# Routed attention and two expert layers: three early steps of the first heads moved to other slots

## Chip, cores and metric

The kernel is one program on one core of a Trainium2 chip. The metric is device time in microseconds (us) of that core; the median of three timed runs of the kernel before is 674.37 us (673.11 to 674.87).

## What is computed

Inputs are q, k, v of shape (2, 8, 768, 64), 16 centroids for each of the 8 heads, and the weights of two expert layers. The part that the change touches is the attention:

```python
q_assign = argmax(normalize(q) @ normalize(centroids), axis=-1)     # a cluster for each row
k_assign = argmax(normalize(k) @ normalize(centroids), axis=-1)
mask   = q_assign[:, :, :, None] == k_assign[:, :, None, :]
scores = where(mask, q @ k.T / 8, -1e9)
scores = scores - max(scores, axis=-1)
attn   = exp(scores) / (sum(exp(scores)) + 1e-9)
out    = attn @ v                                                    # (2, 8, 768, 64)
```

The result, as 1536 tokens of 512 values, then goes through an expert layer with a skip gate and through one with a capacity (8 experts of 512 x 1024 x 512 each). Everything is float32.

## The kernel before, in words

**Tiles.** The 16 (batch, head) pairs are worked as 8 groups g of two heads; head numbers h run from 0 to 15. For a group, `load` (line 108) brings q and k to SBUF (tile `qkn`) and `load_V` (line 123) brings v (tile `vn`); both tiles come from a pool with two buffers, so group 2 gets the buffers of group 0 once every reader of them is done. `prep_T` (128) transposes q and k on TensorE into `qkT`; `prep_H` (153) and `prep_L` (161) split `qkT` into a high part `qkH` and a low part `qkL`, which have one buffer each (pool `wrk`): a group can't write them before all readers of the group ahead are done. For group 1 `prep_H` is on ScalarE and `prep_L` on GpSimd; for groups from 2 on `prep_T` itself writes `qkH` on ScalarE (line 149). `prep_V` (167) splits v: a ScalarE copy to `VA` (line 172) and a GpSimd subtraction to `VL` (line 173), both reading `vn`.

**Stacking.** `stack_q(g, h, t)` (242) copies pieces of `qkH` and `qkL` from SBUF to SBUF into the operands `AA` and `BB` of one head, four DMAs for t = 0 and, for group 0, four more for t = 1 (three for later groups). They are issued by SyncE, but for (0, 1, 0), which GpSimd issues. `stack_mk` does the same for the mask rows.

**Heads.** `mpass(h, c)` (265) computes the row maxima of one block of 128 rows from the t = 0 half of `AA` and `BB`: two matmuls (line 271) and two VectorE reductions (272), and after block 5 one more (274). `mrow(h)` (276) transposes the maxima on TensorE (278) and writes them as rows into `BB` (279), from where `score_mm` (282, matmuls of line 290) subtracts them. `score` (293) takes the exponential on ScalarE (298), splits it (299 on ScalarE, 301 on GpSimd, two buffers for `P`), and `pv` (304) multiplies with `VA` and `VL`.

**Order.** All is put into a table of slots by `at(u, step, ...)`: slot u stands for score block u of 96 (6 for a head), negative slots are the preparation. Slots are emitted in rising u, and within one slot in the order in which `at` was called. The order of TensorE, SyncE, GpSimd and ScalarE is the emitted one throughout; VectorE's is the emitted one up to slot 6 (lines 451 and 452) and is chosen by a planner after that. Each engine works through its instructions in order, and a DMA on SyncE's queue whose condition isn't met holds back all DMAs behind it.

The early slots are: -40 the loads of q and k of groups 0 and 1; -20 the two loads of v and then the whole preparation of group 0, ending with `prep_V(0)`; -10 to -3 the preparation of group 1 (`prep_H` in -6, -5, -4; `prep_L` in -6, -5, -3) beside the row maxima of head 0 (`mpass(0, c)` in slots -8 to -3); -8 also the loads of group 2 (`load(2)`, then `load_V(2)`); -3 also `mrow(0)`; -2 `prep_V(1)`; 0 the first scores. Slot 1 has the stacking of group 1 and slot 3 `prep_mk(1)` (line 239), `stack_mk(1)` and the first `prep_T(2)`.

Of the kernel before, what the change touches and what calls it, by code (L numbers as in the profile page):

```python
# [22 lines left out]
def attention(ctx, tc, q, k, v, centroids, wcat, lgacc, xa, xb, idw, hooks, bind):  # L23
# [354 lines left out]
    def at(u, fn, *a):  # L378
        sched.setdefault(u, []).append((fn, a))
# [1 line left out]
    NH = 2 * NP  # L381
    LM = 8
    MP = (0, 1, 2, 3, 4, 4)
    lead = {1: (-3, -1, -1, 1, 3, 3), 2: (6, 8, 7, 8, 7, 9)}
    for u in range(NH * C):
        h, c = divmod(u, C)
        at(u, score_mm, h, c)
# [21 lines left out]
    for g in range(NP):  # L409
        u = 2 * C * g  # L410
        if g > 1:
            at(u + -32, load, g)
            at(u + -32, load_V, g)
        if g == 0:
            at(-20, load_V, 0)
            at(-20, load_V, 1)
            for x in ((prep_T, 0, 0), (cen_T,), (prep_H, 0, 0), (prep_L, 0, 0), (prep_T, 0, 1), (prep_H, 0, 1), (prep_L, 0, 1),
                      (prep_T, 0, 2), (prep_H, 0, 2), (prep_as, 0, 0), (prep_as, 0, 1), (stack_q, 0, 0, 0), (stack_q, 0, 1, 0),
                      (next, su), (prep_oh, 0, ((0, 1),)), (prep_as, 0, 2), (warm, 5), (prep_mk0, 0), (prep_oh, 0, ((1, 2),)),
                      (prep_L, 0, 2), (warm, 4), (prep_mk0, 1), (warm, 1), (stack_q, 0, 0, 1), (stack_q, 0, 1, 1),  # L420
                      (prep_V, 0)):
                at(-20, *x)
        else:
            w = (-10, -7, -7) if g == 1 else [u + x for x in (-21, -20, -18)]
            for i in range(3):
                at(w[i], prep_T, g, i)
            if g == 1:
                for i, (l, h) in enumerate(zip((-6, -5, -3), (-6, -5, -4))):
                    at(h, prep_H, g, i)
                    at(l, prep_L, g, i)  # L430
            w = (-5, -4, -3) if g == 1 else [u + x for x in (-19, -17, -16)]
            for i in range(3):
                at(w[i], prep_as, g, i)
            w = -1 if g == 1 else u + -14
            at(w, prep_oh, g)
            w = 3 if g == 1 else u + -12
            at(w, prep_mk, g)
            for h in range(2):
                x = 1 if g == 1 else w + 0
                at(x, stack_q, g, h, 0)  # L440
                at(x, stack_q, g, h, 1)
                at(w, stack_mk, g, h)
        if g:
            at(u + -10 if g > 1 else -2, prep_V, g)
        at(u + 2 * C + -3, fin_w, g)
        at(u + 2 * C + 4, fin_den, g)
        at(u + 2 * C + 4, fin_nat, g, 0)
        at(u + 2 * C + 5, fin_nat, g, 1)
# [1076 lines left out]
def tile_kernel(ctx, tc, q, k, v, centroids, moe_w_skip, moe_w_gate, moe_w1, moe_w2,  # L1525
# [6 lines left out]
    with tc.manual_schedule(engines={ET.PE, ET.SP, ET.Pool, ET.Activation}):  # L1532
# [46 lines left out]
        with ExitStack() as actx:  # L1579
            moe.at = actx.enter_context(tc.tile_pool(name="mat", bufs=1))  # L1580
            attention(actx, tc, q, k, v, centroids, wcat, lg, xa, xb, idw, hooks, bind)
# [34 lines left out]
```

## Time and profile before

| | |
|---|---|
| median of three timed runs | 674.37 us |
| the profiled execution, its own time | 678.05 us |
| span of its instructions | 676.3 us |
| mean granted TensorE clock | 0.988 |
| TensorE matmuls busy | 639.2 us (95%) |
| TensorE weight loads busy | 553.2 us (82%) |
| VectorE busy | 419.3 us (62%) |
| ScalarE busy | 379.9 us (56%) |
| GpSimd busy | 264.9 us (39%) |
| DMA, SyncE's queue | 108.18 MB, 52.5% of 16 engines' span |

In the profile PE is TensorE's matmuls and PEld its weight loads, DVE is VectorE, ACT ScalarE, POOL GpSimd and SPq the DMA issues of SyncE. A line of the timeline gives start and duration in us, engine, source line, operation and `out<-in` tiles, and a count where several are merged; in brackets stands how long the engine was idle before and what ended that. The busy shares are means over stages with different limits: the change lies in the first 45 us, and there the stage itself has to be read.

### The profile page before, as it was taken

Reading aid. Unit: us, or ns where it says so; the run is one execution under the profiler, and the core shown is the slowest. Engines: PE = TensorE matmul, PEld = TensorE weight load, DVE = VectorE, ACT = ScalarE, POOL = GpSimd, SP = SyncE. Lnnn points to the kernel's source line nnn. Section 1 sums busy time; section 2 is a strip of 40 time slices with the busy share of each in tenths; the row PEclk is TensorE's granted clock in tenths of the full one; section 3 lists DMA queues with packets and bytes.
Section 4 is the critical chain, followed back from the end, with each engine's and each line's share of the span. In section 5 each row is a group of like instructions: output and inputs, shape, how many; then the busy total and the mean of one; then the engine's idle time right before and its main releaser. Section 6 shows DMA issues by size and latency. Waiting matters only on the chain. (4 is left out here: it accounts for less than half of the span.)

```text
span 676.3 us, 11848 instructions
## 1 busy us (share of the span) xinstructions
PE 639.2 (95%) x4238; PEld 553.2 (82%) x4238; DVE 419.3 (62%) x1027; ACT 379.9 (56%) x626; POOL 264.9 (39%) x194
## 2 busy tenths in 40 slices
PE   7889999999998999999999999997999999999994
PEld 6768888888877888887788899985799889888984
DVE  6958666676678775344867765647454865646421
ACT  4767787878776779841443434323344645546440
POOL 6665776767665688801211112003013212302210
PEclk9899999999998999999999999999999999999998
DMA  8973838484824479420687888941495476367100
GB/s 230 207 145 90 203 85 202 84 201 88 203 63 90 107 176 372 129 77 27 186 317 276 314 321 319 336 152 48 157 389 188 180 277 241 134 244 257 34 32 3
DMA packets 78960, 121.49 MB, mean 180 GB/s; under 512 B 27569, under 2 KB 42929, under 8 KB 78896
## 3 DMA queue, kind: packets, MB, share of 16 engines
q1 hardware_dynamic: 74416, 108.18, 52.5%
q0 software_dynamic: 4480, 12.50, 5.5%
q8 instruction: 35, 0.57, 0.3%
q14 instruction: 29, 0.24, 0.1%
HBM read 87.90 MB, written 13.37 MB: 150 GB/s over the span
## 5 line engine op out<-in xcount | busy, mean ns | idle before, releaser
L301 POOL TENSOR_TENSOR Pl<-P,Ph 128x768 fp32r<-128x768 f32 x93 | 170.3, 1841 | 70.7 <-ACT Ph L299 36.2
L983 DVE TENSOR_TENSOR wl<-l,wh 128x1024 fp32r<-128x1024 f32 x92 | 109.3, 1221 | 51.3 <-ACT wh L982 50.4
L272 DVE TENSOR_REDUCE m<-psx 128x1 f32<-128x384 f32 x192 | 98.0, 551 | 34.4 <-PE psx L271 33.1
L290 PE MATMUL pss<-BB,AA 128*128 128x384 f32 (+1 forms) x384 | 88.9, 355 | 10.4 <-ACT P L298 3.8
L298 ACT ACTIVATE P<-pss 128x384 f32<-128x384 f32 x192 | 84.0, 489 | 24.8 <-PE pss L290 19.8
L982 ACT CAST wh<-l 128x1024 fp32r<-128x1024 f32 x92 | 92.3, 1046 | 0.5 <-DVE acco L1143 0.5
L299 ACT CAST Ph<-P 128x768 fp32r<-128x768 f32 x96 | 80.1, 835 | 4.2 <-PE pso L318 1.2
L1005 PE MATMUL psl<-xt,l 128*128 128x128 f32 x640 | 79.3, 280 | 1.0 <-ACTq L1209 1.0
L290 PEld LDWEIGHTS pss<-BB,AA 128*128 128x128 f32 (+1 forms) x384 | 66.7, 192 | 16.4 <-ACT P L298 5.2
L1005 PEld LDWEIGHTS psl<-xt,l 128*128 128x128 f32 x640 | 76.2, 195 | 2.4 <-ACTq L1209 1.3
L1099 POOL DMA_INDIRECT out_dram<-y,fsi x15 | 15.7, 1047 | 133.5 <-ACT y L1098 126.6
L316 PE MATMUL pso<-Ph,VA 128*65 128x384 f32 x192 | 65.9, 343 | 0.7 <-ACT DN L333 0.7
L318 PE MATMUL pso<-Ph,VL 128*64 128x384 f32 x192 | 66.1, 344 | 0.0
L320 PE MATMUL pso<-Pl,VA 128*65 128x384 f32 x192 | 65.5, 341 | 0.2 <-DVE Pl L301 0.2
L1370 PE MATMUL psl<-xh,wh 128*128 128x256 f32 x224 | 63.1, 281 | 1.8 <-DVE hl L1375 1.8
L1371 PE MATMUL psl<-xl,wh 128*128 128x256 f32 x224 | 62.5, 279 | 0.7 <-DVE xl L1360 0.7
L1372 PE MATMUL psl<-xh,wl 128*128 128x256 f32 x224 | 62.4, 279 | 0.0
L271 PE MATMUL psx<-AA,BB 128*128 128x384 f32 x192 | 52.2, 357 | 3.9 <-DVE m L272 1.4
L1065 PE MATMUL psl<-wh,hh 128*128 128x512 f32 x120 | 48.4, 403 | 0.0
L1091 POOL DMA_INDIRECT xb<-x,fsi x8 | 8.1, 1014 | 101.8 <-DVE x L1090 88.1
L1067 PE MATMUL psl<-wl,hh 128*128 128x512 f32 x120 | 47.1, 393 | 0.0
L1066 PE MATMUL psl<-wh,hl 128*128 128x512 f32 x120 | 47.0, 392 | 0.0
(403 smaller groups left out, 1191.2 us busy)
## 6 DMA issues: line engine op xcount, KB each, us to landing
l<-in_moe_w_dram SPq DMA_DIRECT2D x136, 512.0 KB
AA<-qkH SPq DMA_DIRECT2D x14, 384.0 KB
vn<-in_v_dram SPq DMA_DIRECT2D x8, 384.0 KB
BB<-qkL SPq DMA_DIRECT2D x16, 192.0 KB
xa<-xn SPq DMA_DIRECT2D x8, 384.0 KB
xb<-xn SPq DMA_DIRECT2D x8, 384.0 KB
AA<-qkL SPq DMA_DIRECT2D x31, 96.0 KB
BB<-qkH SPq DMA_DIRECT2D x31, 96.0 KB
```

Of the source, the lines that this page charges most:

```text
L272: nc.vector.tensor_reduce(out=hs[h]["m2"][:, qc, f:f + 1], in_=ps, axis=AX.X, op=ALU.max)
L290: nc.tensor.matmul(ps, AA[0:K, t, kc * 128:(kc + 1) * 128], BB[0:K, t, sl], start=(t == 0), stop=(t == 1))
L298: nc.scalar.activation(out=P[:, f * HF:(f + 1) * HF], in_=ps, func=AF.Exp, scale=1.0 / 8.0)
L299: nc.scalar.copy(Ph, P)
L301: eng.tensor_tensor(out=Pl, in0=P, in1=Ph.bitcast(F32), op=ALU.subtract)
L316: nc.tensor.matmul(o[0:D + 1, :], va, Ph[:, sl], start=(kc == 0), stop=False)
L318: nc.tensor.matmul(o[0:D, :], vl, Ph[:, sl], start=False, stop=False)
L320: nc.tensor.matmul(o[0:D + 1, :], va, Pl[:, sl], start=False, stop=(kc == C - 1))
L982: nc.scalar.copy(h, src)
L983: nc.vector.tensor_tensor(out=l, in0=src, in1=h.bitcast(F32), op=ALU.subtract)
L1005: nc.tensor.matmul(st[k][:, q, :], L1[c][:, f * 128:(f + 1) * 128], xt[:, c, :], start=(c == 0), stop=(c == 3))
L1370: nc.tensor.matmul(ps[:, q, :], wh[:, fs], xh[:, c, :], start=(c == 0), stop=False)
```

## The change

Three things move; no instruction is added or removed. The two loads of v for groups 0 and 1 go from the head of slot -20 to a place behind the t = 0 stacking of both heads. `prep_V(0)` goes from the end of slot -20 to slot -5, behind `mpass(0, 3)` and before the entries of group 1 in that slot. The first row-maximum block of head 1, `mpass(1, 0)`, goes from slot -3 (ahead of `mrow(0)`) to slot -2 (behind `mrow(0)` and `prep_as(1, 2)`).

```diff
-    lead = {1: (-3, -1, -1, 1, 3, 3), 2: (6, 8, 7, 8, 7, 9)}
+    lead = {1: (-2, -1, -1, 1, 3, 3), 2: (6, 8, 7, 8, 7, 9)}
...
         if g == 0:
-            at(-20, load_V, 0)
-            at(-20, load_V, 1)
             for x in ((prep_T, 0, 0), (cen_T,), (prep_H, 0, 0), (prep_L, 0, 0), (prep_T, 0, 1), (prep_H, 0, 1), (prep_L, 0, 1),
                       (prep_T, 0, 2), (prep_H, 0, 2), (prep_as, 0, 0), (prep_as, 0, 1), (stack_q, 0, 0, 0), (stack_q, 0, 1, 0),
+                      (load_V, 0), (load_V, 1),
                       (next, su), (prep_oh, 0, ((0, 1),)), (prep_as, 0, 2), (warm, 5), (prep_mk0, 0), (prep_oh, 0, ((1, 2),)),
-                      (prep_L, 0, 2), (warm, 4), (prep_mk0, 1), (warm, 1), (stack_q, 0, 0, 1), (stack_q, 0, 1, 1),
-                      (prep_V, 0)):
+                      (prep_L, 0, 2), (warm, 4), (prep_mk0, 1), (warm, 1), (stack_q, 0, 0, 1), (stack_q, 0, 1, 1)):
                 at(-20, *x)
+            at(-5, prep_V, 0)
```

## Rows read from the trace of the kernel before

**Rows 1.** Timeline of ScalarE, 15 to 42 us (start, duration, what).
```profile
16.76 0.84 ACT L172 CAST VA<-vn 128x768 fp32r<-128x768 f32 x1
...
22.68 1.66 ACT L157 CAST qkH<-qkT 128x512 fp32r<-128x512 f32 x3 [2.16 <-DVE m L272]
...
25.10 1.28 ACT L298 ACT_TABLE_LOAD   x1
...
35.04 0.99 ACT L239 ACTIVATE MK<-psM,mksc 128x768 fp32r<-128x768 bf16 x1
40.22 0.58 ACT L149 CAST qkH<-psT 128x512 fp32r<-128x512 f32 x1 [4.19 <-DMA AA<-MK]
```

**Rows 2.** Timeline of SyncE's DMA issues, 9 to 45 us.
```profile
9.27 0.57 SPq L250 DMA_DIRECT2D AA<-qkH  x1
...
15.23 0.49 SPq L253 DMA_DIRECT2D BB<-qkL  x1
...
20.80 1.35 SPq L120 DMA_DIRECT2D qkn<-in_k_dram  x2
...
23.63 1.04 SPq L125 DMA_DIRECT2D vn<-in_v_dram  x1
24.77 0.65 SPq L252 DMA_DIRECT2D AA<-qkH  x1
...
35.78 0.68 SPq L255 DMA_DIRECT2D BB<-qkH  x1
```

**Rows 3.** Stretches of 1 us: last two columns are DMA share and GB/s.
```profile
8.00:9.00 1.00, 1.00 (x12) 1.00 (x11) 0.57 (x2) 0.79 (x3) 0.00 (x0) 1.00 1.05 395
...
20.00:21.00 1.00, 1.00 (x11) 1.00 (x9) 0.97 (x3) 0.52 (x1) 0.00 (x0) 1.00 0.62 138
21.00:22.00 1.00, 1.00 (x11) 1.00 (x10) 1.00 (x3) 0.00 (x0) 0.00 (x0) 1.00 0.54 120
...
26.00:27.00 1.00, 1.00 (x5) 1.00 (x4) 0.97 (x3) 0.38 (x1) 1.00 (x1) 0.50 1.01 311
27.00:28.00 1.00, 1.00 (x4) 1.00 (x4) 1.00 (x3) 0.33 (x1) 1.00 (x2) 0.50 1.16 280
28.00:29.00 1.00, 1.00 (x6) 1.00 (x6) 0.77 (x2) 0.82 (x3) 0.75 (x1) 0.79 1.06 171
```

**Rows 4.** Longer stretches, same columns: the part in which DMA is busiest.
```profile
30.00:33.00 3.00, 2.52 (x12) 1.97 (x13) 2.96 (x7) 2.63 (x6) 3.00 (x2) 1.00 1.04 237
...
36.00:38.00 2.00, 1.75 (x13) 1.22 (x11) 0.95 (x1) 0.03 (x1) 1.06 (x1) 1.00 1.02 229
```

**Rows 5.** Timeline of GpSimd, 9 to 45 us.
```profile
17.68 1.68 POOL L173 TENSOR_TENSOR VL<-vn,VA 128x768 fp32r<-128x768 f32 x1 [2.25 <-ACT VA L172]
23.38 3.73 POOL L165 TENSOR_TENSOR qkL<-qkT,qkH 128x512 fp32r<-128x512 f32 x3 [4.01 <-ACT qkH L157]
...
29.74 7.32 POOL L301 TENSOR_TENSOR Pl<-P,Ph 128x768 fp32r<-128x768 f32 x4 [0.99 <-ACT Ph L299]
```

**Rows 6.** Timeline of all engines, 0 to 45 us.
```profile
1.27 0.42 SPq L116 DMA_DIRECT2D qkn<-in_k_dram  x1
...
17.06 0.94 PE L271 MATMUL psx<-AA,BB 128*128 128x384 f32 x4 [0.84 <-DMA BB<-qkH]
...
24.27 0.27 PE L278 MATMUL psR<-idw,m 128*6 128x128 f32 x1 [1.00 <-DVE m L274]
...
24.32 1.02 DVE L272 TENSOR_REDUCE m<-psx 128x1 f32<-128x384 f32 x2
...
25.36 1.63 PE L271 MATMUL psx<-AA,BB 128*128 128x384 f32 x4
```

**Rows 7.** Stretch of 1 us at the start, columns as in Rows 3.
```profile
2.00:3.00 1.00, 1.00 (x7) 1.00 (x6) 0.29 (x1) 0.10 (x1) 0.93 (x7) 1.00 0.61 133
```

**Rows 8.** Timeline of TensorE, 17 to 45 us.
```profile
41.25 1.00 PE L290 MATMUL pss<-BB,AA 128*128 128x384 f32 x4 [1.66 <-ACT P L298]
```

**Rows 9.** Waits, 44 to 80 us (engine, line, for whom: us, times, longest).
```profile
ACT qkH L149 <- DMA AA<-MK: 1.4, 1, 1.4
```

## The prediction

> **What bounds the kernel now.** I read the page first (TensorE 95% busy as a mean) and then only the first 45 us, where the change lies. ScalarE's timeline shows the event that matters: after the mask tile it stands still for 4.19 us and resumes at 40.22 with the first `qkH` cast of group 2 [rows 1]. `qkH` has one buffer, so this cast (line 149) must wait until all 14 stacking DMAs of group 1, which read `qkH` or sit on the same queue, have landed. The exponentials stand behind it on ScalarE, so TensorE waits 1.66 us as well [rows 8], and VectorE and GpSimd have nothing to do. Next I read SyncE's queue: the last of the 14 is issued at 35.78 [rows 2], in a stretch in which the DMA engines are busy throughout (share 1.04 and 1.02 [rows 4]). So in this stage the end is set by DMA: by when the stacking of group 1 can begin behind the loads of group 2, and how fast it runs. What happens on the compute engines before 40.22 has 4.19 us of cover.
>
> The head of the same chain repeats the pattern. ScalarE is idle for 2.16 us before its `qkH` casts of group 1 at 22.68 [rows 1]. The VectorE step named there is a chance neighbour: the casts overwrite the buffer that group 0's stacking reads, and the last of those transfers is issued just before the group 2 loads at 20.80 [rows 2]. Call its landing L; the casts start about 0.3 us after it.
>
> **Part 1, loads of v behind the first stacking.** Two DMAs of 384 KB, 0.786 MB. Before, they follow q and k at once, in the stretch that runs at 395 GB/s [rows 3]: 2.0 us of queue, while nothing else is ready (the first stacking is issued at 9.27 [rows 2]). That place was free. The t = 0 stacking gains at most the 0.84 us for which the first row maximum waits [rows 6], and that gain goes into the cover above: the later casts don't wait for the maxima. After, the 2.0 us lie between the t = 0 and the t = 1 stacking. SyncE's issues of t = 1 don't move, since they wait for `qkL` (15.23 [rows 2]) and the two v issues fit before that; but their bytes queue behind v. The queue has some air there: shares of 0.62 and 0.54 in 20 to 22 us, 0.84 us in all [rows 3]. So L moves by 2.0 - 0.84, about 1.1 us, and the casts from 22.68 to 23.8. Bounds: 0, if v's bytes run beside the stacking, and 2.0, if none of the air is used; I take 1.1, since the air is in rows.
>
> **Part 2, `prep_V(0)` in slot -5.** ScalarE's copy is 0.84 us [rows 1] and GpSimd's subtraction 1.68 us [rows 5], before done at 17.6 and 19.4, where both engines had nothing else. In slot -5 they stand behind `prep_H(1, 0)` and `prep_L(1, 0)`, thus behind L. GpSimd's first `qkL` moves from 23.38 to 24.5; one of the three is 3.73 / 3 = 1.24 us [rows 5], so it ends at 25.7 and `VL(0)` at 27.4. Two things wait for that:
> - GpSimd's own queue: two more `qkL`, `VL(1)`, then the first `Pl`. With 1.1 us of L and 1.68 us of `VL(0)`, less the 0.99 us it was idle, `Pl` starts at 31.5 instead of 29.74 [rows 5]. ScalarE has 0.84 us more before the table load at 25.10 [rows 1]. Together they push the exponentials by about 1.8 us, hidden by the 4.19 us; uncovered it would cost those 1.8.
> - SyncE's queue, which is the price. `load_V(2)` in slot -8 writes into the buffer of group 0's v. Its readers now run until 27.4, while its issue stood at 23.63 [rows 2]. It holds the queue, and the stacking of group 1 (24.77 before) is behind it. From an issue to its bytes takes about 1.1 us (the first k load is issued at 1.27 [rows 6], and the engines fill within 2 to 3 us [rows 7]); so v's bytes begin at 28.5, and 0.393 MB at 311 GB/s [rows 3] end at 29.8. Before, load rates end within 27 to 28 us (311, then 280, then 171 GB/s [rows 3]): between load rates of 311 to 395 and stacking at 171, 280 is a change at 27.5 to 27.8, and I take 27.5, by the higher rate, as small pieces of q and k lie in the 311. The group 1 stacking, whose bytes follow directly, begins 2.3 us later.
>
> From there the stage is the same: 14 transfers, DMA-bound, 12.7 us from 27.5 to the cast at 40.22. The cast comes at 42.5.
>
> **Part 3, `mpass(1, 0)` behind `mrow(0)`.** Its two reductions (1.02 us) leave the place ahead of `mrow(0)`'s write on VectorE [rows 6], so the row of maxima is ready up to 1.0 us earlier. But TensorE's two matmuls used the 1.00 us in which it waits for the maxima [rows 6]; now they come after it, at the low clock (four take 1.63 us against 0.94 [rows 6]), about 0.8 us, ahead of the first scores. Net -0.2 to +0.8, in the cover: nothing.
>
> **Sum.** 0 (parts 1 and 3 before the stall) + 2.3 us. All engines resume from the cast, and the next wait of this kind (1.4 us [rows 9]) lies behind a queue which itself follows the cast, so it moves along. The profiled execution of 678.05 us would be 680.35; it lies 3.7 us over the median of 674.37, so I add to the median: 676.7.
>
> **Rivals.**
> - *v runs beside the stacking.* Loads reach 395 GB/s and stacking 171 to 237 [rows 3, 4], so the stacking may leave engines half used. L then stays, `VL(0)` ends at 26.3, v's bytes at 28.4 (at 395 GB/s) to 28.7: +0.9 to +1.2, 675.4. Against it: the shares are near 1 when stacking alone runs [rows 4]. The Trainium skill (SBUF — State Buffer, Door 1: the DMA port swizzle) says that a DMA's speed depends on how many of 16 ports its partitions reach, and that partitions 0 to 63 reach half of them; stacking writes 64 or 32 partitions and v 128, so by it half of v would find free ports. The rows 3 and 4 agree with the slower stacking, but can't show whether a v behind it in the same queue would overtake.
> - *The stacking of group 1 speeds up* (the one that ends not slower). Before, it starts at 171 GB/s beside the tail of the loads and moves 2.36 MB in about 11.7 us (from 27.5 to some 1 us ahead of the cast), 200 GB/s. After, it starts alone. At 237 GB/s [rows 4] throughout it takes 10.0 us, 1.7 less: +0.6, 675.0; together with the first rival -0.6. It brings the sum under 2.0 us from 207 GB/s on and under zero from 251 GB/s on. Against: the rate also falls later, without loads (1.02 share at 229 [rows 4]).
> - *The clock.* The longer stall leaves TensorE idle for longer, and after the 1.00 us wait at 24.27 its clock stood at 0.50 in 26 to 28 us [rows 3, 6], the 1.2 GHz level. Eight matmuls at that pace cost 1.4 us more than at the full level: 678.1. The Trainium skill (TensorE: Matmul & The Clock Gate, Part 1: The HAM clock gate) calls the low clock the default which activity lifts, and so would expect it after a longer pause. The 1.66 us wait at 41.25 [rows 8] lowered nothing.
> - *The gate isn't there.* If `load_V(2)` didn't wait for `prep_V(0)` (another buffer), only part 1's 1.1 us remain: 675.5. With two buffers and a later reader of the other, I see no way for it.
>
> **How the numbers follow.** Forecast (+1.7 to +3.2, 676.1 to 677.6) 0.46, clock 0.08, v beside 0.24, faster stacking 0.14, no gate 0.08. The bound is 0.3%, 2.0 us, about what a measurement of this kernel tells from no change. Over it lie the clock case and nearly all of the forecast and a little of the others: slower 0.51. Faster by over 2.0 us needs the second rival beyond its row and the first at once, or a kinder VectorE order from slot 7 on, which the planner makes anew: 0.06. The rest, 0.43, is the same. The range goes from 674.2 (faster stacking with v partly beside) to 678.4 (clock).
>
> **What would show it.** The `qkH` casts of group 1 start near 23.8; `load_V(2)` is issued at about 27.4, with a gap in DMA ahead of it; the cast at line 149 comes near 42.5 and TensorE's wait before the scores grows to over 2 us. I am wrong if that cast stays within 41.3, if `load_V(2)` goes out before `VL(0)` ends, or if a later stage gives the shift back.

## The result and the profile after

The changed kernel takes 681.79 us (median of six, 680.52 to 683.52) against 674.92 us of the kernel before in the same series: a ratio of 1.0102 (95% interval 1.0083 to 1.0121), 6.9 us slower. Slower was forecast; the size was not: 2.3 us were forecast, and the time lies outside the range of 674.2 to 678.4.

| | before | after |
|---|---|---|
| median | 674.92 us | 681.79 us |
| the profiled execution, its own time | 678.05 us | 683.52 us |
| span of its instructions | 676.3 us | 681.8 us |
| mean granted TensorE clock of it | 0.988 | 0.979 |
| first `qkH` cast of group 1 (line 157) | 22.68 | 25.77 |
| `load_V(2)` issued (line 125) | 23.63 | 29.45 |
| "the cast" of group 2 (line 149) | 40.22 | 44.53 |
| first evacuation of head 0 (the copy of its result out of the accumulators, line 332) | 52.36 | 58.83 |

From the first evacuation on the two traces run alike (to the 17th evacuation 134.7 us before and 134.6 after), so the whole loss is made in the first 59 us.

ScalarE's timeline of the kernel after, 15 to 62 us (start, duration, what, idle before and what ended it), answers [rows 1]:

```profile
25.77 0.62 ACT L157 CAST qkH<-qkT 128x512 fp32r<-128x512 f32 x1 [5.25 <-DMA qkn<-in_k_dram]
...
38.78 0.99 ACT L239 ACTIVATE MK<-psM,mksc 128x768 fp32r<-128x768 bf16 x1
44.53 0.58 ACT L149 CAST qkH<-psT 128x512 fp32r<-128x512 f32 x1 [4.76 <-DMA AA<-MK]
...
46.66 0.58 ACT L149 CAST qkH<-psT 128x512 fp32r<-128x512 f32 x1
...
52.47 0.59 ACT L149 CAST qkH<-psT 128x512 fp32r<-128x512 f32 x1 [1.95 <-PE psT L147]
...
58.83 0.47 ACT L332 COPY OT<-pso 64x384 f32<-64x384 f32 x1 [1.17 <-PE pso L320]
```

The wait ahead of the casts of group 1 has grown from 2.16 to 5.25 us, the one ahead of the cast from 4.19 to 4.76, and a third wait is new: the last of the three casts of group 2 waits 1.95 us for TensorE's transposes. It comes 7.94 us behind the first. Here are the same casts and the first evacuation in the kernel before, which had no such wait:

```profile
42.35 0.58 ACT L149 CAST qkH<-psT 128x512 fp32r<-128x512 f32 x1
46.11 0.58 ACT L149 CAST qkH<-psT 128x512 fp32r<-128x512 f32 x1
52.36 0.47 ACT L332 COPY OT<-pso 64x384 f32<-64x384 f32 x1 [1.17 <-PE pso L320]
```

There the third cast comes 5.89 us behind the first. SyncE's issues in the kernel after, 9 to 47 us, answer [rows 2]:

```profile
12.66 1.75 SPq L125 DMA_DIRECT2D vn<-in_v_dram  x2
...
19.61 0.54 SPq L255 DMA_DIRECT2D BB<-qkH  x1
20.59 2.00 SPq L120 DMA_DIRECT2D qkn<-in_k_dram  x2
22.64 2.51 SPq L120 DMA_DIRECT2D qkn<-in_q_dram  x2
29.45 0.37 SPq L125 DMA_DIRECT2D vn<-in_v_dram  x1
29.92 0.65 SPq L252 DMA_DIRECT2D AA<-qkH  x1
```

and the queue's own waits, 8 to 45 us (for whom: us, times, longest):

```profile
SPq L125 <- POOL VL L173: 4.2, 1, 4.2
```

`load_V(2)` holds the queue for 4.2 us and waits for `VL(0)`, the subtraction at the end of `prep_V(0)`; the stacking of group 1 goes out behind it. GpSimd's timeline, 15 to 46 us, answers [rows 5]:

```profile
26.47 1.28 POOL L165 TENSOR_TENSOR qkL<-qkT,qkH 128x512 fp32r<-128x512 f32 x1 [10.85 <-ACT qkH L157]
27.71 1.71 POOL L173 TENSOR_TENSOR VL<-vn,VA 128x768 fp32r<-128x768 f32 x1
29.37 2.52 POOL L165 TENSOR_TENSOR qkL<-qkT,qkH 128x512 fp32r<-128x512 f32 x2
31.84 1.71 POOL L173 TENSOR_TENSOR VL<-vn,VA 128x768 fp32r<-128x768 f32 x1
33.47 7.31 POOL L301 TENSOR_TENSOR Pl<-P,Ph 128x768 fp32r<-128x768 f32 x4
```

Stretches of the kernel after (columns as in [rows 3]; the last three are the granted clock, DMA share and GB/s):

```profile
8.00:9.00 1.00, 1.00 (x9) 0.93 (x8) 0.47 (x2) 0.70 (x3) 0.00 (x0) 1.00 0.00 0
17.00:19.00 2.00, 1.94 (x15) 1.91 (x16) 1.60 (x5) 1.05 (x2) 0.00 (x0) 1.00 1.10 336
20.00:21.00 1.00, 1.00 (x11) 1.00 (x9) 0.97 (x3) 0.52 (x1) 0.00 (x0) 1.00 1.06 259
21.00:22.00 1.00, 1.00 (x11) 1.00 (x10) 1.00 (x3) 0.00 (x0) 0.00 (x0) 1.00 1.06 237
23.00:25.00 2.00, 0.73 (x8) 0.74 (x8) 1.53 (x5) 0.00 (x0) 0.00 (x0) 1.00 1.25 196
27.00:29.00 2.00, 2.00 (x8) 2.00 (x8) 2.00 (x5) 1.98 (x5) 2.00 (x2) 0.55 0.09 13
29.00:31.00 2.00, 1.41 (x7) 0.77 (x5) 1.40 (x4) 1.99 (x3) 2.00 (x3) 1.00 0.22 22
48.00:50.00 2.00, 2.00 (x10) 1.91 (x10) 1.49 (x3) 1.94 (x5) 1.70 (x2) 0.50 0.16 9
50.00:52.00 2.00, 2.00 (x10) 1.81 (x10) 0.00 (x0) 0.51 (x1) 2.00 (x2) 0.50 0.26 16
```

Four things are to be seen. The place at 8 to 9 us, where v ran at 395 GB/s before [rows 3], is now empty. From 13 to 27 us the engines are full without a gap (no 1 us stretch under a share of 0.94). From 27 to 31 us, while `load_V(2)` waits and its bytes set out, DMA does almost nothing (share 0.09 and 0.22). And from 48 to 52 us TensorE works without a pause at a granted clock of 0.50, the 1.2 GHz level; the kernel before had 1.00 in every 2 us stretch between 42 and 54. TensorE's row ahead of that, where [rows 8] had 1.66:

```profile
45.56 1.41 PE L290 MATMUL pss<-BB,AA 128*128 128x384 f32 x4 [2.33 <-ACT P L298]
```

### The profile page after: what moved, and what is told of

Same layout as the page of the kernel before. It is cut to its first block, busy times and chain, and to the rows that moved or that the text cites. A ratio compares the mean times of both kernels' runs of the same rounds, so it can differ in the third digit from the quotient of the medians.

```text
span 681.8 us, 11849 instructions
## 1 busy us (share of the span) xinstructions
PE 644.1 (94%) x4238; PEld 556.7 (82%) x4238; DVE 418.7 (61%) x1027; ACT 379.9 (56%) x626; POOL 265.6 (39%) x194
```

## The experiments

**Theory**: (a) v's two loads move the last landing of group 0's stacking, and with it the casts of group 1, by all of their time; (b) `prep_V(0)` then holds `load_V(2)` and the stacking of group 1 back, so that (a) reaches the cast (the gate); (c) the longer stall lets TensorE's clock fall, which costs some 2 us more. **Rivals**: the cost lies in the row maxima that were moved, in GpSimd's chain (`Pl` at 33.47 instead of 29.74), or in the gate alone.

What the traces show of each kernel, in us (after the slash: further traces of the same kernel). "Behind" is the time from the cast to the first evacuation, "low" whether the granted clock fell to 0.50 between the two.

| kernel | ratio | casts g1 | `load_V(2)` issued | the cast | behind | low |
|---|---|---|---|---|---|---|
| before | 1 | 22.68 / 22.26 | 23.63 / 23.20 | 40.22 / 38.48 | 12.14 / 12.15 | no / no |
| after | 1.0102 | 25.77 / 25.37 | 29.45 / 29.04 | 44.53 / 44.23 | 14.30 / 13.98 | yes / yes |
| `prep_V(0)` only (e1, e14) | 1.0056 | 24.09 / 21.98 | 27.75 / 25.62 | 42.16 / 40.18 | 12.15 / 12.14 | no / no |
| loads only (e2, e11, e15, e18) | 1.0056 | 25.47 / 24.97 / 24.50 / 25.59 | 24.87 / 24.45 / 23.98 / 25.07 | 40.68 / 40.23 / 39.77 / 41.16 | 12.13 / 12.15 / 14.61 / 12.15 | no / no / yes / no |
| one load and `prep_V(0)` (e12) | 1.0092 | 24.23 | 27.91 | 42.96 | 14.60 | yes |
| after, row maxima back (e3) | 1.0095 | 24.91 | 28.58 | 43.04 | 13.81 | yes |
| after, `load_V(2)` late (e4) | 1.0045 | 25.11 | 38.76 | 41.21 | 11.51 | no |
| row maxima only (e5) | 0.9999 | 22.96 | 22.87 | 38.53 | 12.14 | no |

**e1, one part alone: `prep_V(0)` in slot -5.**

```diff
-                      (prep_L, 0, 2), (warm, 4), (prep_mk0, 1), (warm, 1), (stack_q, 0, 0, 1), (stack_q, 0, 1, 1),
-                      (prep_V, 0)):
+                      (prep_L, 0, 2), (warm, 4), (prep_mk0, 1), (warm, 1), (stack_q, 0, 0, 1), (stack_q, 0, 1, 1)):
+            at(-5, prep_V, 0)
```

> The kernel before with only prep_V(0) moved to slot -5; v is loaded early as before. Gate theory (load_V(2) must wait for VL(0), which now stands behind the group 1 casts): the casts stay at 22.7 us, VL(0) ends at 26.3, load_V(2) goes out then instead of at 23.6, the DMA queue has a short gap, stacking of group 1 begins about 1.7 us later, the cast at line 149 comes at 41.9 instead of 40.2 and the median rises by 1.7 us, more if TensorE's clock falls after the stall. Queue theory (the loss comes from v's bytes ahead of the t = 1 stacking): no change, cast at 40.2, within 0.5 us of the kernel before.

Measured: 678.24 us, 1.0056 (1.0035 to 1.0077). `load_V(2)` goes out 0.02 us behind the end of `VL(0)`, so the gate is there without the moved loads. The median rose by 4.0 us, where the gate theory had 1.7. The casts stand at 24.09 in this trace, but not by the gate and hardly by the last landing of group 0's stacking: the first loads landed up to 2.6 us late and the t = 0 stacking with them, so TensorE's first row maxima waited for it, and the transposes of group 1 stand behind them. ScalarE's casts follow its copies of these transposes without any idle time:

```profile
19.11 1.12 PE L271 MATMUL psx<-AA,BB 128*128 128x384 f32 x4 [3.63 <-DMA AA<-qkH]
```

```profile
22.83 1.23 ACT L142 COPY qkT<-psT 64x512 f32<-64x512 f32 x2 [1.13 <-PE psT L140]
24.09 0.62 ACT L157 CAST qkH<-qkT 128x512 fp32r<-128x512 f32 x1
```

In the kernel before the same maxima waited 0.84 us [rows 6]. e17, in which nothing of (a) or (b) is changed, has the same wait (3.74 us) and its casts at 24.23, so this comes with the execution and not with the edit. e14 is the same kernel as e1 in a further execution.

> The kernel with only prep_V(0) moved, once more: in its first trace the first loads of q, k and v landed up to 2.6 us later than in before, so its casts of group 1 (24.09) don't show what the edit does. Theory (the edit leaves the landing of group 0's stacking where it was and adds the gate): casts at 22.3 to 23.0, VL(0) end 3.6 us later, 26.0 to 26.6, load_V(2) issued right behind it, cast at line 149 at 40.5 to 41.7, 15 us after that issue. Rival (prep_V(0) itself delays the casts): casts at 24 again.

Measured: 676.50 us in the one run; casts 21.98, `VL(0)` end 25.59, `load_V(2)` 25.62, cast 40.18. So the edit does not delay the casts, and it does set the issue of `load_V(2)` to 3.64 us behind them. Neither trace has the 4.0 us of the median: on average their cast is 1.8 us later than that of the two traces before, and no low clock follows it.

**e2, the other part alone: the loads**, with `prep_V(0)` in slot -6, ahead of everything of group 1, so that no gate can form.

```diff
-            at(-20, load_V, 0)
-            at(-20, load_V, 1)
...
+                      (load_V, 0), (load_V, 1),
...
+            at(-6, prep_V, 0)
```

> The loads of v behind the t = 0 stacking as in the change, but prep_V(0) in slot -6 ahead of prep_H(1, 0), so that it doesn't wait for the stacking of group 0; mpass(1, 0) where it was before. Gate theory: the group 1 casts start at 25.8 us as in the changed kernel, but VL(0) is done by 23, so load_V(2) goes out right behind the group 2 loads, no gap in DMA; stacking begins near 28.5 and the cast at line 149 comes near 41.5 (+1.3), the median +1.3 us. Queue theory: the 3 us by which the casts are late carry through: cast at 43.2 or later, median +3 us or more.

Measured: 678.18 us, 1.0056 (1.0036 to 1.0077). The casts move as in the full change, but `load_V(2)` goes out at 24.87, and the cast comes at 40.68. The median rose by 4.0 us, where the gate theory had 1.3. The profiled execution was the fastest of its kernel (674.80), so the same kernel was traced in further executions:

> The kernel with only the v loads moved, once more. Its first trace was of its fastest execution (674.8 against a median of 678.2). If that trace hid a part of the cost, this one has the cast at line 149 at 42 or later, or a low clock behind it, and a first evacuation at 54.5 or later. If the trace was typical, cast at 40.5 to 41 and first evacuation near 52.8; then the remaining 2 to 3 us of the median lie elsewhere.

> The kernel with only the loads moved, a third time. Two traces had casts at 25.0 and 25.5, the cast at line 149 at 40.2 and 40.7 and no low clock behind it, and both were of executions faster than its median. If the missing 2 to 3 us of the median is a low clock behind the stall that the two executions escaped, this one may show 3.4 or 6.8 us of low clock from 41 to 50 and a first evacuation at 54 to 55, with a time of 677.5 or more.

> The kernel with only the loads moved, a fourth look. Of its three traces two had no low clock behind the stall (674.8 and 676.5, first evacuation 12.1 us after the cast) and one had 6.8 us of it (678.1, 14.6 us after the cast). If the clock behind the stall decides between them, this one falls into one of the two groups: low clock with 677.5 or more, or none with under 677. A run of 678 or more without low clock there would show that something else costs the time.

The name of the last speaks of a filler, but it has none: its edit is that of e2. Measured: 676.53, 678.13 and 676.63 us. Three of the four traces keep the clock behind the cast, and one, e15, doesn't. Its rows, the casts and the evacuation on ScalarE and one stretch:

```profile
39.77 0.59 ACT L149 CAST qkH<-psT 128x512 fp32r<-128x512 f32 x1 [2.91 <-DMA AA<-MK]
...
47.71 0.59 ACT L149 CAST qkH<-psT 128x512 fp32r<-128x512 f32 x1 [1.95 <-PE psT L147]
...
54.38 0.47 ACT L332 COPY OT<-pso 64x384 f32<-64x384 f32 x1 [1.18 <-PE pso L320]
```

```profile
44.00:46.00 2.00, 2.00 (x11) 2.00 (x12) 0.73 (x2) 1.72 (x4) 1.75 (x1) 0.50 0.16 9
```

Its cast is the earliest of the four and its evacuation the latest, with the same 1.95 us wait of the third cast as in the kernel after. Among traces of one kernel the low clock is thus worth 14.61 - 12.14, about 2.5 us at the first evacuation. It is also the only one of the four with a time near the kernel's median. That the other executions near the median lost their time in the same way is likely, but no trace shows it. The clock of the twelve timed executions of e2 points there: the three with a mean granted clock of 0.993 or more took 674.80 to 675.39 us, the nine with 0.990 or less 677.28 to 680.73; where in the execution it was low isn't on record.

**e3, the row maxima put back** into slot -3 in the kernel after, and **e5, the row maxima moved alone** in the kernel before.

```diff
-    lead = {1: (-2, -1, -1, 1, 3, 3), 2: (6, 8, 7, 8, 7, 9)}
+    lead = {1: (-3, -1, -1, 1, 3, 3), 2: (6, 8, 7, 8, 7, 9)}
```

> The changed kernel with mpass(1, 0) back in slot -3. Both theories: as the changed kernel, cast at line 149 at 44.5 us, median within 0.7 us of it (+6 to +7 us against the kernel before), since the row maxima of head 1 lie under the stall. If that move has a price of its own, this kernel is up to 1 us faster than the changed one. Clock theory: its stall is as long, so TensorE's clock falls after it as it did in the changed kernel.

> The kernel before with only mpass(1, 0) moved to slot -2. All theories: the casts of group 1 and the cast at line 149 stay where they are without the other parts (22.7 to 24 us and near 40.2), the first scores come up to 0.8 us later under the stall, the median within 1 us of the kernel before. If the move itself costs, the median rises by 1 us or more although the cast at line 149 stays.

Measured: 680.83 us, 1.0095 (1.0059 to 1.0131), and 674.86 us, 0.9999 (0.9980 to 1.0018). That rival falls: this part costs nothing in either kernel.

**e4, the gate taken away**: `load_V(2)` is issued from slot 2, behind the stacking of group 1.

```diff
-            at(u + -32, load_V, g)
+            at(2 if g == 2 else u + -32, load_V, g)
```

> The changed kernel with one DMA moved: load_V(2) from slot -8 to slot 2, behind the stacking of group 1, so that no stacking waits for VL(0). Gate theory: the group 1 casts stay late at 25.8 us, but the stacking follows them directly (issue near 27.1, bytes from 28.4) and has no v load ahead of it: cast at line 149 at 40.8 to 41.1, median +0.7 us against the kernel before, and no low clock after the stall. Queue theory: the 3 us of the casts carry through, less the 1.3 us of the moved load: cast at 42 to 43, median +2 us or more.

Measured: 676.61 us, 1.0045 (1.0022 to 1.0068). SyncE's issues and ScalarE's casts in its trace:

```profile
27.01 0.65 SPq L252 DMA_DIRECT2D AA<-qkH  x1
...
38.76 0.58 SPq L125 DMA_DIRECT2D vn<-in_v_dram  x1
```

```profile
25.11 0.62 ACT L157 CAST qkH<-qkT 128x512 fp32r<-128x512 f32 x1 [5.18 <-DVE BB L279]
...
41.21 0.59 ACT L149 CAST qkH<-psT 128x512 fp32r<-128x512 f32 x1 [2.09 <-DMA BB<-qkH]
```

The casts of group 1 are as late as in the kernel after (25.11) and `VL(0)` too (28.76), but the stacking now waits for its data alone, 27.01. More than half of the loss is gone, and the clock stays up. This is the run that ties (b) to the loss. It takes away a little more than the gate: the bytes of `load_V(2)` no longer run ahead of the stacking either, 1.3 us by the expectation. The time is 2.4 us over the kernel before, where 0.7 were expected.

**e12, half of (a)**: only group 0's v is moved, `prep_V(0)` and the row maxima as in the change.

```diff
-            at(-20, load_V, 0)
...
+                      (load_V, 0),
...
+            at(-5, prep_V, 0)
```

> The change with only half of it at the queue: the load of v for group 1 stays at the head of the preparation, that of group 0 goes behind the first stacking, prep_V(0) goes to slot -5. If each load of v behind the t = 0 stacking pushes the last landing of group 0's stacking by its own time in the queue, the casts of group 1 stand half way, near 24.0 to 24.3, load_V(2) is issued at 27.6 to 28.0, the cast comes at 41.5 to 42.5, and the time is 1.0 to 1.006 of before. If the first of the two uses the air of 0.84 us that before's trace shows at 20 to 22 us and only the second costs, the casts stand at 22.9 to 23.2 and the time is within that of the kernel where only prep_V(0) is moved, about 1.0056, or less.

Measured: 680.50 us, 1.0092 (1.0072 to 1.0112), casts at 24.23. Against the mean of before's two traces (22.47) one load moves the casts by 1.76 us, two move them by 3.10 (25.57): each is paid in full, and the first doesn't hide in the air at 20 to 22 us. This is one trace, but up to the loads it runs as the second trace before (first stacking issued at 9.14 and 9.15, first row maximum at 16.86 and 16.89). The cast (42.96) and the time came out later than expected, near those of the full change; the low clock is behind the cast here too.

**e6, e7, e8: the cast out of ScalarE's way.** The three `prep_T(2)` go two to three slots later, so that the exponentials don't stand behind the cast; e6 in the kernel after, e7 in the kernel before, e8 in the kernel before together with the edit of e4.

```diff
-            w = (-10, -7, -7) if g == 1 else [u + x for x in (-21, -20, -18)]
+            w = (-10, -7, -7) if g == 1 else [u + x for x in ((-19, -17, -16) if g == 2 else (-21, -20, -18))]
```

> The changed kernel with prep_T(2) two to three slots later (slots 5, 7, 8 instead of 3, 4, 6), so that ScalarE does the exponentials of blocks 4 and 5 before the cast that waits for the stacking. Stall theory (all of the loss is paid at that cast, and the low clock follows from TensorE's wait there): the cast still comes near 43 to 44.5 us, but TensorE's wait there shrinks from 2.3 to 3.1 us to under 1 us, no low clock follows it, and the median falls from 681.8 to 677 or less. If the loss is elsewhere (other waits behind the late casts), the median stays above 680.

> The kernel before with prep_T(2) in slots 5, 7, 8. Stall theory: the cast at line 149 stays at 40.2 us but has two more score blocks ahead of it on ScalarE, TensorE's wait of 1.66 us goes, median 1.5 to 3 us under the kernel before. If TensorE's wait isn't what the cast costs, or prep_T(2) becomes late for head 4's row maxima, no gain or a loss.

> As the run before it, and load_V(2) in slot 2 behind the stacking of group 1. The 384 KB leave the DMA stretch that the cast waits for: cast at line 149 about 1.3 us earlier (38.9), hidden in part by then; median 0 to 1.3 us under the run with prep_T(2) late alone, 2 to 4 us under the kernel before. If the later landing of v for group 2 delays prep_V(2), it is slower than that run.

Measured: e6 680.23 us, 1.0072 (1.0044 to 1.0099); e7 673.88 us, 0.9987 (0.9968 to 1.0006); e8 674.47 us, 0.9988 (0.9970 to 1.0006). All three missed what the stall theory expected: e7 and e8 show no gain that can be told from noise, and e6 stays above 680. So moving the cast out of the way buys nothing in the kernel before; what its stall is worth there these runs don't show, since the later `prep_T(2)` can bring waits of its own. In the kernel after TensorE still stands, now for the stacking itself. Its row in e6:

```profile
44.99 0.98 PE L271 MATMUL psx<-AA,BB 128*128 128x384 f32 x2 [3.39 <-DMA AA<-MK]
```

These are the row maxima of head 2, whose operands come with the last stacking of group 1. So the end of the stage is the stacking, whichever engine is made to wait for it.

**e9, e10: the two kernels in a further execution each**, for the spread of their traces.

> The kernel before once more, for its spread. In its first trace the cast at line 149 came at 40.22, in the trace with only the head's lead moved at 38.53. If that difference is run-to-run spread of the transfers, this run has the cast between 38.3 and 40.3 and a first evacuation between 50 and 52.5 with no low clock after the cast. If the first trace was typical, it stands at 40.0 to 40.5 again. The casts of group 1 stand at 22.6 to 23.0 by either.

> The kernel after once more. Theory (the shift ahead of the stall plus a low clock after it): casts of group 1 at 24.9 to 25.8, VL(0) end 28.5 to 29.5, load_V(2) issued right behind it, cast at 43.0 to 44.6, and about 6.8 us of low clock behind it, first evacuation 14 us after the cast. Rival (the low clock was a chance of the one trace): no low clock behind the cast, first evacuation 12.1 us after it.

Measured: 673.75 and 682.60 us; the rows are in the table. The kernel before has its cast at 40.22 and at 38.48; the first trace was the late one.

**e13, e16, e17: the stall filled with matmuls**, 20 into an unused bank, to keep the clock up without shortening the stall; e13 into a bank of the score pool, e16 into the one of the row of maxima, e17 as e16 in the kernel before.

```diff
+    at(5, warm, 20)
```

```diff
-        ps = ps_w.tile([128, 512], F32, tag="w", name="psR")
+        ps = ps_w.tile([128, 512], F32, tag="w", name="psR"); hs['R'] = ps
...
+    at(5, lambda: [nc.tensor.transpose(hs['R'][:, 0:128], ident, ident) for _ in range(20)])
```

> The kernel after with 20 matmuls into an unused bank (the same that the kernel uses as filler at its start, 0.15 us each, 3.0 us in all) put on TensorE just ahead of the score matmuls that wait in the stall, so TensorE is busy through most of it. They change no result and add work only where TensorE stood still. Theory (the low clock behind the stall costs about 2 us on top of the shift of the cast): the cast stays at 43.0 to 44.6, the clock stays at the full level behind it, the first evacuation comes 12 us after the cast instead of 14, and the time is about 2 us under the 681.8 of after, 679.5 to 680. Rival (the clock is in the cover of another wait): the clock stays up but the time is that of after, 681.5 to 682.5.

> The kernel after with 20 filler matmuls on TensorE in the stall, this time into the bank of the row of maxima, which is free by then (in the earlier filler run the bank was one that the stall itself held, so the filler ran behind the stall and took 4.07 us at the low clock). They write scratch and change no result. Theory (low clock behind the stall costs about 2 us): the filler runs from 42.9 to 45.9, the clock stays at the full level behind it, the first evacuation comes 12 to 12.6 us after the cast instead of 14.3, and the time is 679.5 to 680.5. Rival (the clock is in the cover of another wait): the clock stays up and the time is that of after, 681.5 to 682.5.

> Control: the same filler in the kernel before, whose stall at 41.25 was 1.66 us and lowered nothing. By either theory the filler runs 0 to 1.5 us longer than the stall there, so the time is that of before or up to 1.5 us more, 674.4 to 676; under 673.5 would mean that untraced executions of before also lose time to the clock at this place.

Measured: 683.96 us, 1.0143 (1.0118 to 1.0169); 683.71 us, 1.0130 (1.0105 to 1.0155); 677.16 us, 1.0037 (1.0013 to 1.0061). They decide nothing on (c), since in neither kernel after did the filler run in the stall. TensorE's rows, e13:

```profile
45.53 4.07 PE L60 MATMUL psD<-idw 128*128 128x128 f32 x20 [2.32 <-ACT P L298]
```

and e16:

```profile
44.56 0.97 PE L290 MATMUL pss<-BB,AA 128*128 128x384 f32 x2 [4.52 <-ACT P L298]
...
47.24 2.74 PE L448 MATMUL psR<-idw 128*128 128x128 f32 x20
```

In e13 the bank was one that an exponential behind the cast had to release; in e16 the scores ahead of the filler waited instead, by my reading because the bank of the maxima is kept longer there, which wasn't tested. In e17 the filler ran where the stall had been, and the time rose by 2.7 us all the same. Its trace shows one reason: TensorE waits 2.98 us at 53.43 for VectorE's line 151, a wait that the kernel before hasn't. The planner has put a block of small casts and copies (its lines 535 to 546) ahead of that step on VectorE; in e16 it did the same. So these runs differ from their kernels by more than the filler, and their times can't be read as its price.

## Why the direction was right and the size wrong

With the means of two traces each, the cast moves from 39.35 to 44.38, by 5.0 us, and the time behind it grows from 12.15 to 14.14, by 2.0 us: 7.0 us at the first evacuation, and 6.9 in the medians. The forecast of 2.3 us is thus 4.7 short at the evacuation: 2.0 us are the term L, 2.0 the clock, and 0.7 the base, a first trace before whose stage was longer than that of the second.

- **The term L failed: 1.1 us were put in, 3.1 came** (casts 22.47 to 25.57). The working took 2.0 us for v's bytes, by the 395 GB/s of the start, and took 0.84 us of "air" off. In the new place v's packets run between those of the stacking (336 GB/s in 17 to 19 us). The times of its packets in the trace, which can be told by their 1,536 bytes, add up to 2.8 us of 16 engines (2.7 in the second trace, 1.6 for the one load of e12), against 2.4 at the start. And the air was not to be had: the two 1 us stretches that held it now have shares of 1.06, and at 23 to 25 us the end of the stacking moves at 196 GB/s with a share of 1.25. Nothing but the loads of group 2, issued from 20.59, is in the queue beside it; that these took the air, and the 0.3 us that are left over, is read from the shares and wasn't tested. My upper bound of 2.0 us was too low as well: it priced v at the best rate of the trace, not at that of the place to which it goes.
- **The chain behind L was right.** Casts to the end of `VL(0)`: 3.6 us forecast (23.8 to 27.4), 3.65 and 3.64 measured. `load_V(2)` goes out 0.03 us behind it, as the gate said, and the rival without a gate falls. From that issue to the cast 15.1 us were forecast (27.4 to 42.5) and 15.08 and 15.19 measured. So the cast of the first trace is late by 2.03 against the forecast of 42.5, and L's miss (25.77 - 23.8) is 1.97 of it. Inside these 15.1 two small errors cancelled, which is luck: by the packet times the bytes of `load_V(2)` ended 2.7 us behind its issue (32.13), where I had 2.4 (27.4 to 29.8), and from there to the cast it was 12.4 us, where I had 12.7. The two traces of `prep_V(0)` alone have 14.4 and 14.6 us from that issue to the cast.
- **The clock came on top, not instead.** I gave it 8% as a rival, with the 1.66 us wait that had lowered nothing as the argument against it [rows 8], and no place in the sum. It is a second term: 1.4 us were priced, 2.0 measured (14.14 against 12.15), and its place is the third cast of group 2, which waits for transposes at the low level. That it is the clock is shown by e15 against e2, e11 and e18, which are the same kernel: only e15 has the low level behind the cast, and only e15 takes 14.61 us there; for the kernel after it is read from traces, since the filler runs failed. The Trainium skill (TensorE: Matmul & The Clock Gate, Part 1: The HAM clock gate) calls the low clock the default which activity lifts. The 2.33 us wait and the stretches at 0.50 behind it agree with that, though the length of the wait alone doesn't decide it (last section).
- **v beside the stacking** falls: the casts moved by 3.1 us, and v's packets add up to 2.8. The rule of the Trainium skill (SBUF — State Buffer, Door 1: the DMA port swizzle), by which half of v would find free ports beside the stacking, bought nothing here; besides, two of the four pieces of each stacking write partitions 64 to 95, the other half. The Trainium skill also has a rule that fits (DMA: Bandwidth & Descriptors, Queues, rings and completion order): each engine takes a ring's descriptors in order. The traces agree in that nothing of v, put ahead in the queue, was hidden (1.76 us in e12, 3.1 in the change).
- **A faster stacking** falls: from the last byte of `load_V(2)` to the cast it is 12.4 us in the kernel after and 11.3 in the first trace before (28.88 to 40.22).
- **VectorE's order**, which the planner makes anew, is the same in both kernels but for the moved row maxima and one swapped pair of neighbours near 32 us, well ahead of the cast. Nothing of the loss was seen there.
- **GpSimd's chain** came later than forecast (`Pl` at 33.47, forecast 31.5, by the same miss of L) and stayed hidden: the exponentials still ended ahead of a wait of 4.76 us. **The row maxima** that were moved cost nothing, as forecast (e5: 0.9999): their write starts at 24.65 instead of 25.37.
- **The base.** The cover of 4.19 us, on which I leaned, was measured in a late execution. The second trace has the cast 1.7 us earlier. Adding the shift to the median was right, but the bounds should have held that spread. And that the later casts don't wait for the row maxima, as Part 1 had it, isn't so in every execution: in e1 and e17 they do.

In the medians the parts nearly add up: the loads alone 1.0056, `prep_V(0)` alone 1.0056, both 1.0102. At the cast they don't: it moves by 1.1 us with the loads alone (40.46, mean of four, from 39.35), by 1.8 with `prep_V(0)` alone, and by 5.0 with both, since L reaches the cast in full only through the gate. Why each part alone costs 4.0 us in the median is shown only for the one trace of the loads with the low clock; the rest stays open. None of the kernels tried is clearly faster than the kernel before.

## What to carry to other kernels

A load that "only moves" costs what its bytes take in the company of the new place, and the gaps there may already belong to something that is issued next; price it without credit for gaps, and take what the best rate of the trace gives as the lower bound of the cost, not as the upper one. A reader that is moved later moves the release of its buffer, so look for the load that overwrites the buffer and for what stands behind that load in its queue. And where a stall grows, put the slower clock behind it into the sum as a term with a chance, not among the alternatives to the sum.

## What the runs showed of the hardware

- How long TensorE waited doesn't by itself tell whether its clock falls. Behind its wait for the cast it fell after 1.22 us in e15, and after 2.33 (after), 3.06 (e3), 3.49 (e12) and 3.69 us (e10); it stayed after 1.81 (e2) and 2.02 us (e18). The Trainium skill (TensorE: Matmul & The Clock Gate, Part 1: The HAM clock gate) says that at a kernel's start the number of slow matmuls varies from run to run. The four traces of one kernel show the like behind the cast: one of them has the low level there and three don't.
- The same 20 filler matmuls took 4.07 us in e13, where the clock stood at 0.50 in the 2 us from 46 us, and 2.74 us in e16 and 2.35 us in e17.
- The same kernel's transfers differ by 1.7 us at the cast (40.22 and 38.48), and in the two traces of the kernel with only `prep_V(0)` moved by 2.0 us (42.16 and 40.18): a shift of 1 us in one trace is no finding.
